# Early slots of a gated expert kernel: a second bank for layer 2, weight splits two loads behind, and the first main slot's weights in the early stream

## The chip, the core and the metric

The kernel runs on one core of a Trainium2 chip. Its time is device microseconds of one launch. The kernel before takes 796.64 us, the median of three runs (796.41 to 796.94).

## The reference

Random-feature attention over 8 batches, 8 heads, 576 positions and 64 channels makes x (8 x 576 tokens of 512). A gate then picks one of 8 experts for each token, and the token goes through that expert's two layers.

```python
def phi(x):
    proj = np.einsum('bhsd,df->bhsf', x, w_phi)          # 128 features
    proj = proj - np.max(np.abs(proj), axis=-1, keepdims=True)
    return np.concatenate([np.exp(proj), np.exp(-proj)], axis=-1)
q_p, k_p = (phi(q), phi(k))
kv = np.einsum('bhsf,bhsd->bhfd', k_p, v)
z = np.sum(k_p, axis=2)
x = np.einsum('bhsf,bhfd->bhsd', q_p, kv) / (np.einsum('bhsf,bhf->bhs', q_p, z)[..., None] + 1e-06)
...
for b in range(8):
    prev_e = -1
    for s in range(576):
        fresh_e = int(np.argmax(logits[b, s]))           # logits = x @ w_gate
        e = fresh_e if s == 0 or local_gate[b, s] < 0.5 else prev_e
        prev_e = e
        p = softmax(logits[b, s])
        h = np.maximum(x[b, s] @ w1[e], 0.0)             # 512 -> 1024
        out[b, s] = p[e] * (h @ w2[e])                   # 1024 -> 512
```

## The kernel before, in words

**Three parts.** The attention front takes two batches at a time (`bp` 0 to 3) and leaves x in DRAM. The gate of a pair counts tokens per expert and scatters each token's number and probability into a list in DRAM (`lst`), ordered by expert. The expert part works in *slots*: a slot is one expert and 256 tokens of its list (`n=(2,)`, two units of 128 tokens), or 512 (`n=(2, 2)`, a quad, which is two groups of 256), or 128.

**Early and main slots.** Three slots are planned before all tokens are counted: two after the second pair, one after the third (`EARLY = 3`, `HALFWAY = 2`). They are named E1, E2 and E3 here (`e0`, `e1`, `f0` in the code). TensorE works on them from about 316 us, when the front is done, to about 396 us; in this time the last pair's gate and the plan of the main slots (`plan_main`) run on VectorE and GpSimd. The plan comes in two steps, both called `more()` from layer 2: the arithmetic and the read of the list (L619), and then two transposes on TensorE that turn the list (L632). Main slots follow; M1 and M2 are the first two, both quads, M1 of expert rows that the plan names.

**A slot.** Its tokens are gathered from DRAM (GpSimd), transposed on TensorE (`tokens`, L914) and written as xhi (ScalarE, L923) and xlo (VectorE, L924). fp32 products are made of three fp32r matmuls, high by high (L928), low by high (L929) and high by low (L930). Layer 1 makes four tiles, each of two of the eight blocks of hidden features, in two banks of `psl` by turns; each is evicted as hh (ScalarE, L963) and hl (VectorE, L964). Layer 2 makes one tile (128 tokens x 512) for each unit; VectorE scales it by the probability (y, L1015) and GpSimd scatters it to the output (L1018). Until the front's pools are closed, layer 2's tiles all use one bank, `psm4`; M1 and later slots have two more (`psr`).

**Weights.** A slot has eight pieces of 128x1024 fp32 (512 KB), four for each layer. SyncE loads a piece into a raw buffer (L851; the expert number is read into a SyncE register first). There are three raw buffers (`mxg`), and from `open_rest` on, that is from M1 on, another three (`ml1`) by turns. A loaded piece is *split*: ScalarE casts it to whi (L861), VectorE subtracts for wlo (L862; for E1, GpSimd). Split pieces take a place in a ring of 12, from `open_rest` on 13.

**The order of loads and splits.** `spare()` starts the next piece of the next slot when a place of the ring will be free: load, then split. It is called through `used()` each time a piece has been used up. `slots()` runs a list of slots; `self.coming` holds those whose pieces are still to come. The early slots are one such list and the main slots another, so M1's pieces start only after the last early slot's code. Each engine takes its instructions in one order, fixed when the kernel is built: a scheduler picks them by priority and by when operands should be there, so code order is not the order on an engine. `tc.issue_after(x)` forbids it to place an instruction ahead of x.

Of the kernel before, what the change touches and what calls it, by code (L numbers as in the profile page):

```python
# [27 lines left out]
WAIT = 4  # L28
PLACE = 16
LAG = 1  # L30
WE, WR, WL = 8, 4, 1
FILL = 6
KVLAG = 1
# [16 lines left out]
class Kernel:  # L50
# [9 lines left out]
    def run(self):  # L60
        nc, tc, A = self.nc, self.tc, self.A
        act, dve = self.act, self.dve
        with ExitStack() as root:
# [77 lines left out]
                for _ in self.last_gate:  # L141
                    pass
            no = lambda: None
            self.slots(self.eslots, soon=[no, self.fetched_last, go, no, go, no, go, rest], later=[[no, no, more]] * 2)
            back.close()
            self.open_rest(root)
            self.moe()
# [716 lines left out]

    def spare(self):

        while self.coming:
            s = self.coming[0]
            i = len(s.get("w", ()))
            if i == 8:  # L870
                self.coming.pop(0)
                continue
            if self.held < sum(n for _, n in self.wphases):
                self.load(s, i)
                self.split(s)
                self.held += 1
            return

    def used(self, n):
        for _ in range(n):  # L880
# [62 lines left out]
    def layer1(self, s, gi, between, soon=()):  # L943

        pe, act, dve = self.pe, self.act, self.dve
        xh, xl = s["x"][gi]
        w, last = s["w"], gi == len(s["n"]) - 1
        hp = self.ml1 if gi else self.mx2
        hh = hp.tile([128, 8, 256], F32R, name="hh", bufs=1)
        hl = hp.tile([128, 8, 256], F32R, name="hl", bufs=1)  # L950
        s.setdefault("h", []).append((hh, hl))
        if s["n"][gi] == 2:
            for f2 in range(4):
                t = self.psl.tile([128, 2, 256], F32, name="l1")
                wh, wl = w[f2]
                for j in (0, 1):
                    for d in range(4):
                        c = slice(d * 256 + j * 128, d * 256 + j * 128 + 128)
                        self.three(t[:, j, :], wh[:, c], wl[:, c], xh[:, d, :], xl[:, d, :], d == 0, d == 3)
                    if soon:  # L960
                        soon[2 * f2 + j]()
                hc = slice(2 * f2, 2 * f2 + 2)
                act.activation(hh[:, hc, :], t, AF.Relu)  # L963
                dve.scalar_tensor_tensor(hl[:, hc, :], t, 0.0, hh[:, hc, :].bitcast(F32), ALU.max, ALU.subtract)  # L964
                if between:
                    between.pop(0)()
                if last:
                    self.used(1)
                else:
                    self.spare()  # L970
            return []

        hs = self.ml1.tile([128, 1024], F32, name="hs", tag="hh", bufs=1)
        x = slice(0, 128)

        def turn(q):
            tt = self.turned()
            for j in (0, 1):
                f = q * 2 + j
                pe.transpose(tt[:, j, :], hs[:, f * 128:f * 128 + 128], self.ident)  # L980
            hc = slice(q * 2, q * 2 + 2)
            self.parts(s, hh[:, hc], hl[:, hc], x, tt[:, 0:2])
        for q in range(4):
            t = self.psl.tile([128, 256], F32, name="l1")
            for d in range(4):
                self.both(s, q, t, xh[:, d, x], xl[:, d, x], slice(d * 256, d * 256 + 256), d == 0, d == 3)
                if d == 0 and q > 1:
                    turn(q - 2)
            act.activation(hs[:, q * 256:(q + 1) * 256], t, AF.Relu)
            if between and q in (0, 2):  # L990
                between.pop(0)()
            self.used(1)
        return [lambda: turn(2), lambda: turn(3)]

    def layer2(self, s, gi, between, held=None):
# [2 lines left out]
        u0 = s["u"] + sum(s["n"][:gi])  # L998
        for k in range(s["n"][gi]):
            self.l2n = getattr(self, "l2n", 0) + 1  # L1000
            p = self.psr if hasattr(self, "psr") and self.l2n % 3 else self.psm4
            t = p.tile([128, DM], F32, name="l2")
            o = slice(k * 128, k * 128 + 128)
            for f in range(8):
                c = slice((f % 2) * DM, (f % 2) * DM + DM)
# [6 lines left out]
                    self.spare()  # L1012
            y = self.mx2.tile([128, DM], F32, name="yl", bufs=1) if held is not None else self.mx2.tile([128, DM], F32, name="y")
            u = u0 + k
            dve.tensor_scalar_mul(y, t, s["prob"][:, u:u + 1])  # L1015

            def put(y=y, at=s["tok"][:, u:u + 1]):
                ins = pool.indirect_dma_start(self.A["out"], bass.IndirectOffsetOnAxis(at, 0), y, None,  # L1018
# [8 lines left out]
    def slots(self, order, held=None, soon=(), later=()):  # L1027
        first = order[0]
        for g in range(len(first["n"])):
            for f in self.tokens(first, g):  # L1030
                f()
        self.held = len(first.get("w", ()))
        self.coming = list(order)
        for i, s in enumerate(order):
            while len(s.get("w", ())) < 8:
                self.spare()
            new = order[i + 1] if i + 1 < len(order) else None
            last = len(s["n"]) - 1
            for gi in range(last):
                self.layer1(s, gi, [])  # L1040
            between = self.tokens(new, 0, bool(soon) and i == 0) if new else []
            rest = self.layer1(s, last, between, () if i else soon)
            if i < len(later):
                rest = list(later[i])
            for f in between:
                f()
            for gi in range(last + 1):
                self.layer2(s, gi, rest, None if new else held)
            if new and len(new["n"]) == 2:
                for f in self.tokens(new, 1):  # L1050
                    f()
            s.clear()
# [135 lines left out]
```

## Time and profile before

| | us | share of the span |
|---|---|---|
| median of three runs | 796.64 | |
| profiled execution | 796.07 | |
| its span, first to last instruction | 794.0 | |
| TensorE busy | 767.4 | 97% |
| VectorE busy | 511.2 | 64% |
| ScalarE busy | 401.9 | 51% |
| GpSimd busy | 158.0 | 20% |

Times in views of the trace count from the start of the span. PE is TensorE's matmul, PEld its weight load, DVE VectorE, ACT ScalarE, POOL GpSimd, SPq SyncE's queue. A row of a timeline holds start, duration, engine, line, operation, written tile <- read tiles, sizes, count, and in brackets the idle time ahead of it and what ended it (a line name stands there for the operation that released it). L12 is line 12 of the kernel. A row of the windows view holds the stretch and its length, then for PE, PEld, DVE, ACT and POOL the busy time with the number of instructions, then the granted TensorE clock as a share of the full one, the share of DMA busy, and GB/s. A row of the waits view names who waits, for what, and then total time, count and longest wait. In a trace the layer tiles are all called `l` and the transposed tokens `tr`.

### The profile page before, as it was taken

To read this page: it belongs to the slowest core of one execution; us is meant where nothing else is said; L and a number is where in the kernel's file an instruction comes from. 1 tells how busy PE (TensorE), PEld (TensorE's weight loads), DVE (VectorE), ACT (ScalarE), POOL (GpSimd) and SP (SyncE) were. 2 spreads that over 40 slices of the span, in tenths; PEclk is the share of its full clock that TensorE was granted. 3 is DMA by queue.
4 is the path that set the end of the run, shared out by engine and by line. 5 is a ranking of instruction groups with operands and counts; after the bars stand their busy time and mean duration, and the time that the engine had idled before them with its cause. 6 is when DMAs were issued, how large, how long until landed. Compare 5 with 4: busy or idle time off the path is not lost.

```text
span 794.0 us, 23193 instructions
## 1 busy us (share of the span) xinstructions
PE 767.4 (97%) x9674; PEld 676.2 (85%) x9674; DVE 511.2 (64%) x939; ACT 401.9 (51%) x708; POOL 158.0 (20%) x166
## 2 busy tenths in 40 slices
PE   6999999999999999999899999999999999999993
PEld 5899988988888989988798997698988987689882
DVE  4677798789878886985742225544866824768621
ACT  4666566666687665544531114433745713757410
POOL 0000001200275132166121102102321311110100
PEclk9999999999999999999999999999999999999997
DMA  7655454454687721747922695733966679959300
GB/s 200 195 163 155 116 146 128 135 139 122 172 264 208 223 77 42 225 148 277 333 83 88 261 347 180 258 120 114 362 204 201 244 262 410 358 188 321 111 27 14
DMA packets 77227, 151.29 MB, mean 191 GB/s; under 512 B 8524, under 2 KB 50828, under 8 KB 77078
## 3 DMA queue, kind: packets, MB, share of 16 engines
q1 hardware_dynamic: 67424, 127.33, 49.6%
q0 software_dynamic: 7424, 20.08, 7.1%
q10 hardware_dynamic: 2272, 2.37, 0.9%
q8 instruction: 77, 1.26, 0.7%
q14 instruction: 30, 0.25, 0.1%
HBM read 128.21 MB, written 22.06 MB: 189 GB/s over the span
## 4 chain that ended last, share of the span: by engine, by line
PE 84%; DVE 5%; DMA 4%; issue 2%; ACT 1%; SPq 1%; another core or an unknown queue 0%; POOLq 0%; POOL 0%; DVEq 0%
PE l L928 15%; PE l L930 15%; PE l L929 15%; PE kvp L255 9%; PE nm L314 9%; PE pj L213 9%; PE qt L233 4%; PE l L941 4%; DMA wraw<-in_w1h 3%; PE tr L914 2%; DVE m L216 1%; PE nm L293 1%; DVE sb L218 1%; PE nm L281 1%; PE tr L980 1%
## 5 line engine op out<-in xcount | busy, mean ns | idle before, releaser
L861 ACT CAST whi<-wraw 128x1024 fp32r<-128x1024 f32 x136 | 142.2, 1048 | 155.9 <-PE l L930 68.9
L862 DVE TENSOR_TENSOR wlo<-wraw,whi 128x1024 fp32r<-128x1024 f32 x128 | 156.2, 1222 | 75.4 <-ACT whi L861 73.7
L928 PE MATMUL l<-xhi,whi 128*128 128x256 f32 x512 | 146.2, 285 | 1.0 <-DVE hl L964 1.0
L930 PE MATMUL l<-xhi,wlo 128*128 128x256 f32 x512 | 143.7, 281 | 0.0
L929 PE MATMUL l<-xlo,whi 128*128 128x256 f32 x512 | 143.6, 281 | 0.0
L216 DVE TENSOR_REDUCE m<-pj 128x8 f32<-128x1024 f32 x72 | 87.8, 1220 | 47.4 <-PE pj L213 46.8
L928 PE MATMUL l<-whi,hh 128*128 128x512 f32 x288 | 114.5, 398 | 2.7 <-DVE y L1015 1.7
L930 PE MATMUL l<-whi,hl 128*128 128x512 f32 x288 | 113.2, 393 | 0.6 <-DVE hl L964 0.6
L929 PE MATMUL l<-wlo,hh 128*128 128x512 f32 x288 | 112.7, 391 | 0.0
L236 ACT ACTIVATE qp<-qt 128x512 f32<-128x512 f32 x144 | 84.7, 604 | 52.5 <-PE qt L233 52.0
L222 ACT ACTIVATE kp<-sb 128x512 f32<-128x512 f32 x144 | 82.8, 622 | 50.4 <-DVE sb L218 44.1
L928 PEld LDWEIGHTS l<-xhi,whi 128*128 128x128 f32 x512 | 96.8, 189 | 3.5 <-DVE hl L964 1.5
L929 PEld LDWEIGHTS l<-xlo,whi 128*128 128x128 f32 x512 | 96.8, 189 | 0.4
L930 PEld LDWEIGHTS l<-xhi,wlo 128*128 128x128 f32 x512 | 96.9, 189 | 0.1
L213 PE MATMUL pj<-first,kq 64*128 64x128 f32 x1152 | 85.5, 289 | 6.8 <-DMA kq<-in_kqT 6.8
L218 DVE TENSOR_TENSOR sb<-pj,m 128x1024 f32<-128x1024 f32 x72 | 88.1, 1224 | 4.0
L1018 POOL DMA_INDIRECT out<-y,p_tokm x31 | 39.2, 1263 | 244.2 <-DVE y L1015 243.6
L314 PE MATMUL nm<-kvs,qp 128*64 128x74 f32 x2304 | 86.7, 228 | 0.3
L213 PEld LDWEIGHTS pj<-first,kq 64*128 64x128 f32 x1152 | 71.5, 191 | 12.1 <-issue 4.6
L314 PEld LDWEIGHTS nm<-kvs,qp 128*64 128x64 f32 x2304 | 79.3, 136 | 1.4 <-ACT kvs L295 0.5
L255 PE MATMUL kvp<-v,kp 128*64 128x65 f32 x2048 | 77.3, 225 | 0.0
L255 PEld LDWEIGHTS kvp<-v,kp 128*64 128x64 f32 x2048 | 67.7, 139 | 5.9 <-issue 5.7
(229 smaller groups left out, 1028.1 us busy)
## 6 DMA issues: line engine op xcount, KB each, us to landing
wraw<-in_w1h SPq DMA_DIRECT2D x68, 512.0 KB, 5.3
wraw<-in_w2h SPq DMA_DIRECT2D x68, 512.0 KB, 5.1
kq<-in_kqT SPq DMA_DIRECT2D x47, 384.0 KB, 3.9
v<-in_va SPq DMA_DIRECT2D x48, 195.0 KB, 3.7
xs<-xo SPq DMA_DIRECT2D x48, 128.0 KB, 2.4
whi<-in_w1h SPq DMA_DIRECT2D x8, 512.0 KB, 4.3
wlo<-in_w1h SPq DMA_DIRECT2D x8, 512.0 KB, 5.0
whi<-in_w2h SPq DMA_DIRECT2D x8, 512.0 KB, 10.4
```

Source lines behind the costliest of these rows:

```text
L213: self.last_pe = self.pe.matmul(t[:, h, i % 2, j, :], kq[r, j, s], self.w2[r], start=True, stop=True)
L216: dve.tensor_reduce(m, f, AX.X, ALU.max, apply_absolute_value=True)
L218: self.last_dve = dve.tensor_sub(sb.rearrange("p h c j f -> p (h c j) f"), f, m.unsqueeze(2).broadcast_to([128, 8, 128]))
L222: self.last_act = act.activation(kp[:, :, :, sg, :].rearrange("p c h f -> p h c f"), sb[:, :, :, 0], AF.Exp, scale=1.0 - 2 * sg)
L236: self.act.activation(qp[:, sg], t, AF.Exp, scale=1.0 - 2 * sg)
L255: self.pe.matmul(self.kvp[r, sg, h], self.ch[i]["kp"][:, h, sg, r], self.v(i, b)[:, h], start=first and n < 2, stop=last and n >= 6)
L314: self.pe.matmul(e["t"][r, c - c0, h, :], self.ch[i]["qp"][:, sg, h, q0 + r.start:q0 + r.stop], kvs[:, sg, h, :], start=sg == 0, stop=sg == 1)
L861: self.act.copy(hi, raw)
L862: (low or self.dve).tensor_sub(lo, raw, hi.bitcast(F32))
L928: mm(o, ah, bh, start=first, stop=False)
L929: mm(o, ah, bl, start=False, stop=False)
L930: self.last_pe = mm(o, al, bh, start=False, stop=last)
```

## The change

1. *Second bank.* In the early slots the first unit's layer-2 tile stays in `psm4`; the second unit's goes to `psb`, a bank of the attention front (tag `nm`) that is idle by then.
2. *Splits two loads behind.* `spare()` now queues each loaded piece in `pending` and splits it when `MLAG = 2` later loads have been issued (or, when nothing is left to load, one at each call). In the early slots a split is also bound to come after the latest hh and after the latest hl or y that the code has reached (`issue_after`). For the main slots the lag is 0, as before. A piece takes its place in the ring's count at its load.
3. *M1 in the early stream.* After the second step of the plan, called from E2's layer 2, M1 is added to `self.coming` of the early list, so its pieces follow E3's through the three raw buffers of `mxg`.

```diff
+MLAG = 2
...
-            self.slots(self.eslots, soon=[no, self.fetched_last, go, no, go, no, go, rest], later=[[no, no, more]] * 2)
+            def last():
+                more()
+                self.coming.append(self.qs[0])
+            self.last_h, self.last_d, self.pending = self.last_act, self.last_dve, []
+            self.slots(self.eslots, soon=[no, self.fetched_last, go, no, go, no, go, rest],
+                       later=[[no, no, more], [no, no, last]])
...
     def spare(self):
+        got = False
         while self.coming:
             s = self.coming[0]
-            i = len(s.get("w", ()))
+            i = len(s.get("w", ())) + len(s.get("raw", ()))
             if i == 8:
                 self.coming.pop(0)
                 continue
             if self.held < sum(n for _, n in self.wphases):
                 self.load(s, i)
+                if s["raw"]:
+                    self.pending.append(s)
+                self.held += 1
+                got = True
+            break
+        while len(self.pending) > (self.lag if got else max(len(self.pending) - 1, 0)):
+            s = self.pending.pop(0)
+            with ExitStack() as st:
+                if self.lag:
+                    st.enter_context(self.tc.issue_after(self.last_h.ins))
+                    st.enter_context(self.tc.issue_after(self.last_d.ins))
                 self.split(s)
-                self.held += 1
-            return
...
-                act.activation(hh[:, hc, :], t, AF.Relu)
-                dve.scalar_tensor_tensor(hl[:, hc, :], ...)
+                self.last_h = act.activation(hh[:, hc, :], t, AF.Relu)
+                self.last_d = dve.scalar_tensor_tensor(hl[:, hc, :], ...)
...
-            p = self.psr if hasattr(self, "psr") and self.l2n % 3 else self.psm4
-            t = p.tile([128, DM], F32, name="l2")
+            if hasattr(self, "psr"):
+                p, kw = self.psr if self.l2n % 3 else self.psm4, {}
+            else:
+                p, kw = (self.psb, dict(tag="nm")) if k else (self.psm4, {})
+            t = p.tile([128, DM], F32, name="l2", **kw)
...
-            dve.tensor_scalar_mul(y, t, s["prob"][:, u:u + 1])
+            self.last_d = dve.tensor_scalar_mul(y, t, s["prob"][:, u:u + 1])
...
-        self.held = len(first.get("w", ()))
+        self.held = len(first.get("w", ())) + len(first.get("raw", ()))
         self.coming = list(order)
+        self.lag = MLAG if soon else 0
```

The change lengthens the file, so a line of before stands some 8 to 24 lines later after it (L632 becomes L640, L862 L870, L924 L944, L928 to L930 L948 to L950, L964 L984, L1015 L1039).

**Where instructions move.** Three places, each before and after. In these rows a number behind a tile's name tells one tile of a name from another; it differs between the two programs for the same tile.

TensorE, E2's layer 2, at the end of its first unit. Before, `l_6723` is E3's first layer-1 tile and `l_6684` E2's second unit:

```order
L930 MATMUL l_6723<-xhi,wlo 128x256
L928 MATMUL l_6723<-xhi,whi 128x256
L929 MATMUL l_6723<-xlo,whi 128x256
L928 MATMUL l_6684<-whi,hh 128x512
L929 MATMUL l_6684<-wlo,hh 128x512
L930 MATMUL l_6684<-whi,hl 128x512
L632 MATMUL pt<-first,lr 128x40 x2
```

After, `l_6646` is E2's first unit, `l_6684` its second:

```order
L949 MATMUL l_6646<-wlo,hh 128x512
L950 MATMUL l_6646<-whi,hl 128x512
L948 MATMUL l_6646<-whi,hh 128x512
L949 MATMUL l_6646<-wlo,hh 128x512
L950 MATMUL l_6646<-whi,hl 128x512
L950 MATMUL l_6684<-whi,hl 128x512
L640 MATMUL pt<-first,lr 128x40 x2
L948 MATMUL l_6684<-whi,hh 128x512
```

Before, E3's first layer-1 tile filled the place between the two units, and the plan's transposes (L632) stood inside the second unit. After, the second unit follows the first directly, the transposes stand right behind its start, and all of E3's layer 1 comes after it.

VectorE, E3's layer 1. Before, `wlo_6962` and the further splits are M1's pieces, and `hl_6722` is E3's hidden tile:

```order
L862 TENSOR_TENSOR wlo_6962<-wraw_6959,whi_6961 128x1024
L964 SCALAR_TENSOR_TENSOR hl_6722<-l1_6723,hh_6721 128x512
L862 TENSOR_TENSOR wlo_6968<-wraw_6965,whi_6967 128x1024
L862 TENSOR_TENSOR wlo_6974<-wraw_6971,whi_6973 128x1024
L964 SCALAR_TENSOR_TENSOR hl_6722<-l1_6750,hh_6721 128x512
L862 TENSOR_TENSOR wlo_6980<-wraw_6977,whi_6979 128x1024
L862 TENSOR_TENSOR wlo_6986<-wraw_6983,whi_6985 128x1024
L964 SCALAR_TENSOR_TENSOR hl_6722<-l1_6777,hh_6721 128x512
```

After, `y_6741` is E2's second unit, the splits are M1's, and `hl_6747` is E3's hidden tile:

```order
L1039 TENSOR_SCALAR y_6741<-l2_6684,p_probe_4777 128x512
L870 TENSOR_TENSOR wlo_6726<-wraw_6707,whi_6725 128x1024
L870 TENSOR_TENSOR wlo_6738<-wraw_6715,whi_6737 128x1024
L984 SCALAR_TENSOR_TENSOR hl_6747<-l1_6748,hh_6746 128x512
L870 TENSOR_TENSOR wlo_6778<-wraw_6723,whi_6777 128x1024
L984 SCALAR_TENSOR_TENSOR hl_6747<-l1_6781,hh_6746 128x512
L870 TENSOR_TENSOR wlo_6811<-wraw_6735,whi_6810 128x1024
L984 SCALAR_TENSOR_TENSOR hl_6747<-l1_6814,hh_6746 128x512
```

Before, two splits stand between one hl and the next; after, two ahead of the first hl and one between the others.

VectorE, from E3's layer 2 to M1. Before, `l2_6831` and `l2_6861` are E3's two units, `xlo_6913` and `xlo_6929` M1's first and second 256 tokens; `wlo_7075`, `wlo_7108`, `wlo_7141` and `wlo_7042` take the places of E3's last four pieces:

```order
L862 TENSOR_TENSOR wlo_7075<-wraw_7072,whi_7074 128x1024
L1015 TENSOR_SCALAR y_6856<-l2_6831,p_probf_6045 128x512
L924 TENSOR_TENSOR xlo_6913<-tr_6914,xhi_6912 128x4x128
L924 TENSOR_TENSOR xlo_6913<-tr_6921,xhi_6912 128x4x128
L862 TENSOR_TENSOR wlo_7108<-wraw_7105,whi_7107 128x1024
L862 TENSOR_TENSOR wlo_7141<-wraw_7138,whi_7140 128x1024
L862 TENSOR_TENSOR wlo_7193<-wraw_7190,whi_7192 128x1024
L1015 TENSOR_SCALAR y_6886<-l2_6861,p_probf_6045 128x512
L924 TENSOR_TENSOR xlo_6929<-tr_6930,xhi_6928 128x4x128
L924 TENSOR_TENSOR xlo_6929<-tr_6937,xhi_6928 128x4x128
L862 TENSOR_TENSOR wlo_7042<-wraw_7039,whi_7041 128x1024
```

After, `l2_6880` and `l2_6918` are the two units, `xlo_6970` M1's first 256 tokens (two tiles), and the splits are those that take the places of E3's last pieces (`wlo_7075` to `wlo_7042`) and one more of M2 (`wlo_7233`):

```order
L870 TENSOR_TENSOR wlo_6892<-wraw_6874,whi_6891 128x1024
L1039 TENSOR_SCALAR y_6913<-l2_6880,p_probf_6045 128x512
L870 TENSOR_TENSOR wlo_7075<-wraw_7072,whi_7074 128x1024
L870 TENSOR_TENSOR wlo_7108<-wraw_7105,whi_7107 128x1024
L870 TENSOR_TENSOR wlo_7141<-wraw_7138,whi_7140 128x1024
L1039 TENSOR_SCALAR y_6943<-l2_6918,p_probf_6045 128x512
L944 TENSOR_TENSOR xlo_6970<-tr_6978,xhi_6969 128x4x128
L870 TENSOR_TENSOR wlo_7042<-wraw_7039,whi_7041 128x1024
L870 TENSOR_TENSOR wlo_7233<-wraw_7230,whi_7232 128x1024
L944 TENSOR_TENSOR xlo_6970<-tr_6971,xhi_6969 128x4x128
```

Before, the first 256 tokens of M1 were ready for matmuls between E3's two units; after, both their tiles come behind the second unit's y, and two splits stand between them.

More of the change, by code (lines that the diff above doesn't have):

```diff
@@ L962, in layer1 @@
                 hc = slice(2 * f2, 2 * f2 + 2)
-                act.activation(hh[:, hc, :], t, AF.Relu)
-                dve.scalar_tensor_tensor(hl[:, hc, :], t, 0.0, hh[:, hc, :].bitcast(F32), ALU.max, ALU.subtract)
+                self.last_h = act.activation(hh[:, hc, :], t, AF.Relu)
+                self.last_d = dve.scalar_tensor_tensor(hl[:, hc, :], t, 0.0, hh[:, hc, :].bitcast(F32), ALU.max, ALU.subtract)
                 if between:
```

## Prediction

> **What bounds the kernel now.** I read the page first (busy shares and the chain that ended last), then busy time by window around the early slots, then the timeline of each engine from 316 to 400 us.
>
> ```profile
> span 794.0 us, 23193 instructions
> PE 767.4 (97%) x9674; PEld 676.2 (85%) x9674; DVE 511.2 (64%) x939; ACT 401.9 (51%) x708; POOL 158.0 (20%) x166
> PE 84%; DVE 5%; DMA 4%; issue 2%; ACT 1%; SPq 1%; another core or an unknown queue 0%; POOLq 0%; POOL 0%; DVEq 0%
> 340.00:360.00 20.00, 19.10 (x131) 17.35 (x130) 17.91 (x76) 10.91 (x14) 13.01 (x12) 1.00 0.56 187
> 360.00:380.00 20.00, 17.84 (x118) 15.84 (x117) 10.60 (x13) 7.39 (x8) 9.79 (x8) 1.00 0.78 280
> 380.00:400.00 20.00, 18.79 (x110) 15.67 (x109) 15.29 (x18) 12.02 (x15) 6.06 (x6) 1.00 0.88 319
> 500.00:600.00 100.00, 99.98 (x668) 88.69 (x665) 58.51 (x66) 46.74 (x64) 20.26 (x16) 1.00 0.61 207
> ```
>
> TensorE (first number after the comma) is full from 500 us on, so a microsecond gained before M1 starts reaches the end undiminished, and nothing after it can be gained. Between 340 and 400 us it idles 0.90 + 2.16 + 1.21 = 4.3 us: that is what the change can win. Where:
>
> ```profile
> 349.56 0.47 PE L928 MATMUL l<-whi,hh 128*128 128x512 f32 x1 [0.90 <-DVE p_rim L607]
> 363.96 0.50 PE L928 MATMUL l<-whi,hh 128*128 128x512 f32 x1 [1.21 <-DVE y L1015]
> 378.43 0.38 PE L928 MATMUL l<-xhi,whi 128*128 128x256 f32 x1 [0.95 <-DVE hl L964]
> 387.15 0.50 PE L930 MATMUL l<-whi,hl 128*128 128x512 f32 x1 [0.63 <-DVE hl L964]
> 389.75 0.51 PE L928 MATMUL l<-whi,hh 128*128 128x512 f32 x1 [0.53 <-DVE y L1015]
> 395.18 0.39 PE L930 MATMUL l<-whi,hl 128*128 128x512 f32 x1
> 395.42 1.03 PE L914 MATMUL tr<-first,xg 128*128 128x128 f32 x8
> 396.20 0.37 PE L928 MATMUL l<-xhi,whi 128*128 128x256 f32 x1
> 345.00 1.20 DVE L862 TENSOR_TENSOR wlo<-wraw,whi 128x1024 fp32r<-128x1024 f32 x1
> 348.68 0.73 DVE L1015 TENSOR_SCALAR y<-l,p_probe 128x512 f32<-128x512 f32 x1
> 349.40 0.67 DVE L964 SCALAR_TENSOR_TENSOR hl<-l,hh 128x512 fp32r<-128x512 f32 x1
> 362.02 1.22 DVE L862 TENSOR_TENSOR wlo<-wraw,whi 128x1024 fp32r<-128x1024 f32 x1 [0.87 <-ACT whi L861]
> 363.16 0.74 DVE L1015 TENSOR_SCALAR y<-l,p_probe 128x512 f32<-128x512 f32 x1
> 376.54 1.23 DVE L862 TENSOR_TENSOR wlo<-wraw,whi 128x1024 fp32r<-128x1024 f32 x1 [1.07 <-ACT whi L861]
> 377.68 0.69 DVE L964 SCALAR_TENSOR_TENSOR hl<-l,hh 128x512 fp32r<-128x512 f32 x1
> ```
>
> All five waits are for VectorE, which is late because a result (y, hl) stands behind a weight split (L862), and the split behind its load. At 363.96 and 389.75 the wait is for the one layer-2 bank; at 378.43 and 387.15 for hl behind a split. The last PE row is the first matmul of M1, 396.20: the point that the change must move. Counted from matmul start to matmul start (a restart also costs 0.1 to 0.2 us) the five take 1.1, 1.4, 1.1, 1.3 (E3's layer 2 has a second, shorter one) and 0.8 us.
>
> **The change part by part.** No instruction is added or removed on any engine; order, banks and buffers change.
>
> *Second bank.* E2's and E3's second units go to the other bank, so the waits of 363.96 and 389.75 go: 1.4 + 0.8, and about 0.3 of restarts. The first, at 349.56, only changes its name. The order now puts two matmuls of E2's second unit ahead (0.5 us done early), then the third layer-1 tile, which needs hl of the first; that hl stands behind three splits and a y as before (345.00 to 349.40), because the planning arithmetic in front of them waits for the same counts. I take it as unmoved: at best it goes (-1.1), at worst the split that now stands inside that arithmetic delays it by one split (1.2).
>
> *Splits two loads behind.* E3's eight splits keep their places up to 363 us; two of them and all of M1's follow later. E3's first loads move behind SyncE's register loads of the plan (from 331 to 347 us). That costs nothing: layer 1 of E3 starts near 367 and the pieces are split by then; without that cover it would be 16 us.
>
> *M1's pieces in the early stream.* These rows say when they come now, and how long a load takes:
>
> ```profile
> 319.35 0.36 SPq L851 DMA_DIRECT2D wraw<-in_w1h  x1
> 322.91 1.05 ACT L861 CAST whi<-wraw 128x1024 fp32r<-128x1024 f32 x1 [0.83 <-DMA wraw<-in_w1h]
> 365.39 2.04 SPq L851 DMA_DIRECT2D wraw<-in_w1h  x4
> 370.64 1.05 ACT L861 CAST whi<-wraw 128x1024 fp32r<-128x1024 f32 x1 [0.27 <-DMA wraw<-in_w1h]
> 375.46 1.05 ACT L861 CAST whi<-wraw 128x1024 fp32r<-128x1024 f32 x1 [1.24 <-DMA wraw<-in_w1h]
> 375.50 8.39 SPq L851 DMA_DIRECT2D wraw<-in_w1h  x4
> SPq L851 <- PE pt L632: 2.0, 1, 2.0
> SPq L851 <- DMA lr<-lst,p_rim: 1.0, 1, 1.0
> 358.48 1.31 POOL L619 DMA_INDIRECT lr<-lst,p_rim  x1 [0.31 <-issue]
> 364.85 0.41 PE L632 MATMUL pt<-first,lr 40*128 40x40 f32 x2
> ```
>
> M1's first load waited for the plan's transposes (L632) and left at 365.39. Alone, a load takes 3.6 us to its cast (319.35 to 322.91). In the burst of 365.39 the second (issued 0.6 later) takes 4.7, the fourth (issued at about 367.1) 8.4. In the change each load leaves when one of three raw buffers is free, so at most three are in flight, beside the token gathers: between 3.6 and 8.4, and I take 4.6, nearest to the second of the burst. [...]
>
> With 4.6 the splits follow each other by some 2.5 us: the last of E3's at 367.0, M1's first (free at 363.2, loaded by 367.0, behind a y) at 369.2, M1's second (issued 365.2, cast 369.8 to 370.9) at 372.0. The hl of E3's first layer-1 tile stands right behind that one: ready at 372.7, where TensorE wants its bank at 372.4. So of the 1.1 us of 378.43, 0.8 is won. The hl's of the later tiles come in time, so 387.15 goes: 1.3. The plan's transposes are now reached near 361.6; the list landed at about 363.3 before (SyncE's 2.0 us wait for L632 began there), issued at 358.48. The scatters start some 1.5 us earlier and the list read 3 to 4, so I take no wait; with the list unmoved it costs 1.7.
>
> So E3's layer 2 ends at 395.42 - (0.5 + 1.4 + 0.8 + 1.3 + 0.8 + 0.3) = 390.3 and, since the eight transposes between its units (0.8 by the 395.42 row) now stand behind it, at 389.5.
>
> *The boundary to M1* takes much of this back. Before, the first 256 tokens were turned between the two units and their parts were ready at 391. Now all are turned after both, and VectorE's order is: third released split, y, first xlo, two more splits, second xlo.
>
> ```profile
> 391.46 1.05 ACT L861 CAST whi<-wraw 128x1024 fp32r<-128x1024 f32 x1 [1.56 <-PE l L930]
> 395.66 1.05 ACT L861 CAST whi<-wraw 128x1024 fp32r<-128x1024 f32 x1 [0.33 <-PE l L930]
> 396.61 1.06 ACT L923 CAST xhi<-tr 128x512 fp32r<-128x512 f32 x2
> 395.36 1.23 DVE L862 TENSOR_TENSOR wlo<-wraw,whi 128x1024 fp32r<-128x1024 f32 x1 [0.21 <-ACT whi L861]
> 396.51 0.75 DVE L1015 TENSOR_SCALAR y<-l,p_probf 128x512 f32<-128x512 f32 x1
> 397.22 1.29 DVE L924 TENSOR_TENSOR xlo<-tr,xhi 128x512 fp32r<-128x512 f32 x2
> ```
>
> These casts wait for the second unit's matmuls to free E3's pieces, 1.4 us apart (391.46, then two more, then 395.66), the last 0.5 us after the last matmul began. In the change the fourth starts at 389.7, the third at 388.3, whose split takes VectorE to 390.5. Then y to 391.2; the first xlo to 392.0 (its cast, behind the fourth, ends at 391.3); two splits at 1.15 to 394.2; the second xlo to 394.9; four transposes more on TensorE (0.4) and M1's layer 1 goes on at 395.4. By then two of its matmuls (0.24) and four transposes of M2 (0.4) are done. The second of the two splits needs M2's sixth load, issued when M1's last split ends (about 384.8) with four ahead: landed near 390.3, cast by 392.4, in time by 0.7 us.
>
> Sum: 396.2 + 0.6 - 395.4 = 1.4 us. The profiled execution took 796.07 us, of which the span is 794.0, so 794.7; it lay 0.57 under the median of the runs, so 795.2. About 0.2% (1.6 us) is what a measurement of this kernel can tell from no change: the forecast lies just inside.
>
> **The rivals.**
> - *More is won.* Either the wait of 349.56 goes with the others (1.1), or M2's two splits don't hold the second xlo (2.3: it would follow the first). For: VectorE is idle for most of the 10 us that follow its split at 331 in the new order, so the planning could begin earlier. Against: its counts come from TensorE's place, which moves little, and the order fixes the two splits. Gain 2.5 to 4.8, centre 793.3.
> - *No change to be seen.* The loads come 1.4 us later than I put them, by slower transfers beside the gathers or by the list unmoved. For: the burst's third and fourth loads. Gain 0 +- 0.8: 796.6.
> - *Slower: the three raw buffers become the bound.* M1 had six buffers before, three of them opened by the release of the old pools; now three carry it. If a round trip is the 8.4 us of the burst, M1's second split ends 3.8 us later, TensorE waits that long for hl in E3's layer 1, and the later tiles add a little. From 6.0 us the gain is gone, from 7.6 it is slower by over 0.2%; at 8.4, 2.4 us: 799.0. Against: the burst had up to six weight loads in flight, not three.
> - *The lag does nothing.* If splits stay where they are, only the banks and the boundary count: that is the forecast with the 1.1 us of 378.43 kept, within the second rival.
>
> **How the numbers follow.** Forecast 0.45 (gain 0.6 to 2.2, 794.4 to 796.0), more is won 0.20, no change 0.23, slower 0.12. Faster by over 0.2% is the whole of "more is won" and not quite half of the forecast: 0.40; slower by over 0.2% 0.12; the rest, 0.48, lies within. The range leaves out the best part of the first rival and most of the third: 793.0 to 798.0.
>
> **What would show it.** In the profile after: no wait of PE for y at E2's and E3's second units; the wait near 350 us now on hl; one short wait for hl in E3's layer 1; M1's loads from about 363 us; E3's last layer-2 matmul near 389.2; then a wait of some 3.8 us in all around M1's transposes, on DVE, with M1's layer 1 running from 395.4. Casts waiting for DMA far beyond 5 us after the issue, with PE waiting for hl by 2 us or more, would show the third rival; a first layer-1 matmul of M1 well under 394, the first.

## The result and the profile after

The changed kernel takes 801.4 us, the median of eight runs (799.31 to 805.26); the kernel before took 796.94 beside it. The ratio is 1.0067 (95% interval 1.0052 to 1.0082): slower by some 0.7%, 5 us, where 1.4 us less was forecast. The profiled execution took 805.26 us, the slowest of the eight; its span is 9.3 us longer than that of before. So its waits show the mechanism, and their sum is that of a bad run.

The page's first line and the windows around the early slots, after (columns as before):

```profile
span 803.3 us, 23192 instructions
340.00:360.00 20.00, 18.83 (x134) 17.31 (x133) 17.55 (x77) 8.96 (x11) 12.64 (x12) 1.00 0.62 191
360.00:380.00 20.00, 16.58 (x101) 13.91 (x100) 11.41 (x14) 9.58 (x11) 9.04 (x8) 1.00 0.87 275
380.00:400.00 20.00, 15.90 (x87) 13.32 (x85) 13.88 (x14) 11.11 (x13) 1.98 (x2) 1.00 0.93 326
400.00:420.00 20.00, 18.97 (x138) 18.68 (x139) 8.22 (x12) 5.54 (x10) 4.87 (x5) 0.83 0.36 118
```

From 340 to 400 us TensorE idles 8.7 us (before: 4.3), in the next 20 us another 1.0, and there the granted clock is 0.83. Timeline of TensorE, its waits and the row that takes M1's layer 1 up for good:

```profile
351.56 0.39 PE L948 MATMUL l<-xhi,whi 128*128 128x256 f32 x1 [1.17 <-DVE hl L984]
362.55 0.51 PE L948 MATMUL l<-whi,hh 128*128 128x512 f32 x1 [1.03 <-ACT hh L983]
363.91 0.50 PE L950 MATMUL l<-whi,hl 128*128 128x512 f32 x1 [0.63 <-DVE hl L984]
378.12 0.39 PE L948 MATMUL l<-xhi,whi 128*128 128x256 f32 x1 [1.76 <-DVE hl L984]
381.72 0.39 PE L948 MATMUL l<-xhi,whi 128*128 128x256 f32 x1 [0.51 <-DVE hl L984]
400.15 0.33 PE L934 MATMUL tr<-first,xg 128*128 128x128 f32 x1 [3.74 <-DVE y L1039]
403.62 1.12 PE L934 MATMUL tr<-first,xg 128*128 128x128 f32 x4 [0.88 <-DVE xlo L944]
404.39 0.56 PE L949 MATMUL l<-xlo,whi 128*128 128x256 f32 x1
```

The waits for y between the units of E2 and E3, and those for hl inside E3's layer 2, are gone. In their place stand one for hh and one for hl in E2's layer 2, two for hl in E3's layer 1, and 4.6 us around M1's transposes. Their causes are in the order of ScalarE and VectorE and in the loads (an SPq row can hold several issues and starts at the first; 369.51 is the second of the four of 367.51):

```profile
355.02 0.33 SPq L859 DMA_DIRECT2D wraw<-in_w1h  x1
367.51 7.39 SPq L859 DMA_DIRECT2D wraw<-in_w1h  x4
369.51 0.33 SPq L859 DMA_DIRECT2D wraw<-in_w1h  x1
387.44 3.27 SPq L859 DMA_DIRECT2D wraw<-in_w1h  x4
360.95 1.05 ACT L869 CAST whi<-wraw 128x1024 fp32r<-128x1024 f32 x1 [2.54 <-DMA wraw<-in_w1h]
361.90 0.59 ACT L983 ACTIVATE hh<-l 128x512 fp32r<-128x512 f32 x1
375.15 1.05 ACT L869 CAST whi<-wraw 128x1024 fp32r<-128x1024 f32 x1 [1.89 <-DMA wraw<-in_w1h]
394.36 1.05 ACT L869 CAST whi<-wraw 128x1024 fp32r<-128x1024 f32 x1 [2.07 <-DMA wraw<-in_w1h]
397.13 1.99 ACT L869 CAST whi<-wraw 128x1024 fp32r<-128x1024 f32 x2 [0.23 <-DMA wraw<-in_w1h]
376.23 1.23 DVE L870 TENSOR_TENSOR wlo<-wraw,whi 128x1024 fp32r<-128x1024 f32 x1 [1.70 <-ACT whi L869]
377.38 0.68 DVE L984 SCALAR_TENSOR_TENSOR hl<-l,hh 128x512 fp32r<-128x512 f32 x1
396.93 2.50 DVE L870 TENSOR_TENSOR wlo<-wraw,whi 128x1024 fp32r<-128x1024 f32 x2 [0.27 <-ACT whi L869]
399.35 0.75 DVE L1039 TENSOR_SCALAR y<-l,p_probf 128x512 f32<-128x512 f32 x1
```

Three pictures of the same thing: something that TensorE waits for stands on its engine behind a split whose load has not landed. At 361 us it is E2's last hh, behind E3's fourth piece, which found a raw buffer only at 355.02 and was cast 5.9 us later. At 377 it is E3's hl behind M1's second piece, issued at 369.51 and cast 5.6 us later. At the boundary it is y behind three splits of M2, whose first load left at 387.44 and was cast 6.9 us later. In each case the load both left late and took longer than alone (3.6 us in the kernel before, 319.35 to 322.91). And then the clock:

```profile
398.00:400.00 2.00, 0.00 (x0) 0.00 (x0) 1.95 (x3) 1.61 (x3) 0.00 (x0) 1.00 1.03 336
400.00:402.00 2.00, 1.85 (x13) 1.85 (x13) 2.00 (x4) 1.93 (x3) 1.32 (x2) 0.72 0.95 334
406.00:408.00 2.00, 2.00 (x13) 2.00 (x12) 0.08 (x1) 0.00 (x0) 0.46 (x1) 0.57 0.78 215
408.00:410.00 2.00, 2.00 (x20) 2.00 (x19) 0.43 (x1) 0.60 (x1) 0.00 (x0) 1.00 0.18 72
```

Behind the wait of 3.74 us the granted clock is 0.50 for 6.8 us, until about 407.7. From 404.39 to 407.73 TensorE starts 15 matmuls of layer 1 in 3.34 us, the next 15, at 1.00, in 1.77: by an estimate from these two 1.6 us are lost. Layer 1 of M1 goes on 8.2 us later than before (404.39 against 396.20) with two matmuls done (0.24): 8.2 - 0.2 + 1.6 = 9.6, near the 9.3 of the spans.

### The profile page after: what moved, and what is told of

The parts are those of the page before. It is cut to its first block, busy times and chain, and to the rows that moved or that the text cites. A ratio compares the mean times of both kernels' runs of the same rounds, so it can differ in the third digit from the quotient of the medians.

```text
span 803.3 us, 23192 instructions
## 1 busy us (share of the span) xinstructions
PE 771.7 (96%) x9674; PEld 679.9 (85%) x9674; DVE 512.2 (64%) x939; ACT 402.0 (50%) x708; POOL 156.4 (19%) x166
## 4 chain that ended last, share of the span: by engine, by line
PE 82%; DVE 6%; DMA 5%; issue 2%; ACT 2%; SPq 1%; POOL 0%; another core or an unknown queue 0%; POOLq 0%; ACTq 0%; DVEq 0%
PE l L948 15%; PE l L950 14%; PE l L949 14%; PE kvp L263 9%; PE nm L322 9%; PE pj L221 8%; PE qt L241 4%; PE l L961 4%; DMA wraw<-in_w1h 2%; PE tr L934 2%; DMA wraw<-in_w2h 2%; DVE wlo L870 1%; DVE m L224 1%; PE nm L301 1%; ACT whi L869 1%
## 5 line engine op out<-in xcount | busy, mean ns | idle before, releaser
L870 DVE TENSOR_TENSOR wlo<-wraw,whi 128x1024 fp32r<-128x1024 f32 x128 | 156.2, 1223 | 77.3 <-ACT whi L869 75.7
L948 PE MATMUL l<-xhi,whi 128*128 128x256 f32 x512 | 147.3, 288 | 3.5 <-DVE hl L984 3.4
L950 PE MATMUL l<-xhi,wlo 128*128 128x256 f32 x512 | 144.3, 282 | 0.0
L948 PE MATMUL l<-whi,hh 128*128 128x512 f32 x288 | 114.2, 397 | 1.0 <-ACT hh L983 1.0
L950 PE MATMUL l<-whi,hl 128*128 128x512 f32 x288 | 113.2, 393 | 0.6 <-DVE hl L984 0.6
L948 PEld LDWEIGHTS l<-xhi,whi 128*128 128x128 f32 x512 | 97.6, 191 | 6.3 <-DVE hl L984 4.3
L950 PEld LDWEIGHTS l<-xhi,wlo 128*128 128x128 f32 x512 | 97.5, 190 | 0.0
L984 DVE SCALAR_TENSOR_TENSOR hl<-l,hh 128x512 fp32r<-128x512 f32 x64 | 43.9, 686 | 49.4 <-ACT hh L983 49.3
```

The source lines that it names most:

```text
L870: (low or self.dve).tensor_sub(lo, raw, hi.bitcast(F32))
L948: mm(o, ah, bh, start=first, stop=False)
L950: self.last_pe = mm(o, al, bh, start=False, stop=last)
```

## The experiments

Ratios are to the kernel before, run beside on the same chip. The runs fell on chips of two kinds: on some the kernel before takes 796 to 797 us, on two 809 to 810. On these TensorE idles near 350 us without a cause that the profile names (below), and ratios from there are not compared with those of the others. e11, e1b and e3b are e11b, e1 and e3 on the second of these two.

| run | what it is | before, us | kernel, us | ratio (95%) |
|---|---|---|---|---|
| first comparison | the change | 796.94 | 801.40 | 1.0067 (1.0052 to 1.0082) |
| again | the change | 796.25 | 803.40 | 1.0100 (1.0080 to 1.0120) |
| e8_hold | + M2's splits bound (VectorE) | 796.25 | 799.35 | 1.0054 (1.0034 to 1.0074) |
| e9_lag0_hold | the same, no lag | 796.25 | 801.37 | 1.0077 (1.0057 to 1.0097) |
| e7_idle | the kernel before, TensorE held up | 796.25 | 819.40 | one run |
| again2 | the change | 796.16 | 802.84 | 1.0079 (1.0061 to 1.0096) |
| e11b_hold2 | + M2's splits bound (both engines) | 796.16 | 797.56 | 1.0018 (1.0007 to 1.0029) |
| e14_late_m1 | e11b + 5 raw buffers, M1's splits late | 796.16 | 796.48 | 1.0003 (0.9989 to 1.0018) |
| e15_best | e14, E1 to E3 split at once, plan's second step later | 796.16 | 801.88 | 1.0066 (1.0047 to 1.0086) |
| e10_raw5_hold2 | e11b + 5 raw buffers | 796.13 | 794.34 | **0.9974** (0.9962 to 0.9986) |
| e16_six | e14, six of M1's splits before M1, plan's second step later | 796.13 | 795.85 | 0.9990 (0.9979 to 1.0002) |
| e1_bank | bank alone | 810.01 | 812.45 | 1.0024 (1.0007 to 1.0042) |
| e2_lag0 | the change, no lag | 810.01 | 811.99 | 1.0024 (1.0009 to 1.0039) |
| e3_nojoin | the change, M1 not joined | 810.01 | 811.35 | 1.0018 (1.0001 to 1.0036) |
| e5_raw5 | the change, 5 raw buffers | 810.01 | 811.16 | 1.0017 (1.0002 to 1.0032) |
| e11_hold2 | as e11b | 808.78 | 808.00 | 0.9993 (0.9972 to 1.0013) |
| e12_bank_hold2 | bank + M2's splits bound | 808.78 | 809.61 | 1.0012 (0.9998 to 1.0026) |
| e1b_bank | bank alone | 808.78 | 812.58 | 1.0036 (1.0021 to 1.0051) |
| e3b_nojoin | as e3 | 808.78 | 811.08 | 1.0025 (1.0005 to 1.0044) |

again2, e11b, e14, e15, e10 and e16 ran on the same chip.

**One part less.** e1_bank is the kernel before with the diff's bank lines; the others are the change with

```diff
-MLAG = 2                                # e2_lag0
+MLAG = 0
-                self.coming.append(self.qs[0])          # e3_nojoin
+                pass
-        rp = self.ml1 if hasattr(self, "ml1") and self.rk % 2 else self.mxg      # e5_raw5
+        m = [0, 2][hasattr(self, "mraw")]     # mraw: two more, from open_main on
+        rp = self.mraw if self.rk % (3 + m) >= 3 else self.mxg
```

> The kernel before with the second bank alone (the early slots' second unit in the idle bank; loads, splits and M1 as before). If the bank was sized rightly and the loss lies in the loads, the two waits for y (1.21 and 0.53 us) go and the kernel takes 794.5 to 796.3 us. If the bank itself does the harm (units run ahead and their results pile up on VectorE at the boundary to M1), it takes 797.5 us or more.

> The changed kernel with MLAG = 0: each piece is split right behind its load and bound to nothing; the bank and M1's early loads stay. If the lag and its bindings are the cause, E3's first loads leave near 331 us again, the waits near 362 us (1.03 and 0.63) go and it takes 796.5 to 798 us. If the three raw buffers are the cause whatever the lag, M1's loads still take 7 to 9 us each and it stays within 1.5 us of 801.4.

> The changed kernel without its third part: M1 stays out of the early list; bank, lag and bindings stay. If M1's loads through three raw buffers are the cause, M1's loads leave in a burst near 365 us, the two waits for hl in E3's layer 1 (1.76 and 0.51) go, the wait at the boundary is under 2 us, the clock stays at 1.00 and it takes 796 to 798 us. If the lag is the cause, it takes 799.5 us or more.

> The changed kernel with five raw buffers instead of three from the end of the attention front on (two new ones, in place of the three that M1 and later slots had besides). If the number of buffers holds M1's loads back, each load leaves some 5 us earlier, the waits for hl in E3's layer 1 go, and it takes 796 to 798.5 us. If the transfers themselves are the limit (they share the DMA engines with the gathers), more in flight only makes each longer and it stays within 1.5 us of 801.4.

These four ran on a chip of the other kind, and separate nothing: they lie within 0.0007 of each other. The timeline of TensorE (e1_bank) shows how the chip differs, with idle time that no operation ends (`issue`: the view names nothing that TensorE waited for):

```profile
352.22 0.28 PE L930 MATMUL l<-xhi,wlo 128*128 128x256 f32 x1 [1.03 <-issue]
```

One thing they do say: the bank alone is no gain there (1.0024, and 1.0036 in e1b, where 0.999 to 1.001 was expected). In both e1 and e1b y stands behind M2's splits at the boundary, a wait of 1.2 us.

**The boundary.** e8 binds M2's splits (`last_x` is M1's latest xlo), e9 has MLAG = 0 besides, and e7 prices the clock:

```diff
+                elif s is self.qs[1]:                                    # e8, e9
+                    st.enter_context(self.tc.issue_after(self.last_x.ins))
-            self.dve.tensor_sub(lo[:, :, o], ...)                        # e7, on the kernel before
+            more = dict(m8=6, m12=9, m14=12, m16=15).get(s["name"], 0) if o.start == 128 else 0
+            for _ in range(1 + more):
+                self.dve.tensor_sub(lo[:, :, o], ...)
```

> The changed kernel once more, unedited, to stand beside the variants on their chip. By either theory its ratio to the kernel before is 1.005 to 1.008 as in the first comparison. If the loss depends on where the loads, the gathers and the plan happen to meet on a chip, the ratio differs from chip to chip by more than the intervals.

> The changed kernel with one more binding: M2's splits may not stand ahead of M1's xlo on an engine (issue_after the last xlo of M1), so at the boundary VectorE's order is y, y, four xlo, then M2's splits. Theory boundary: M2's splits, which wait for loads of 7 us, stand ahead of y and of the xlo that TensorE waits for (3.74 and 0.88 us) and the long wait halves the granted clock for 8 us. Then the two waits shrink to under 1.5 us together, the clock stays 1.00 and the time falls to 796.5 to 798 (ratio 1.000 to 1.0015). Rival, raw buffers: M1 has too few pieces for layer 1 at that point anyway, the wait only changes its name, ratio 1.004 or more.

> As the last one, and with MLAG = 0, so that E3's loads leave near 331 us again and M1's follow them at once: bank, M1 in the early list and the binding of M2's splits stay. Theory boundary plus late loads: both causes are gone, the bank's gain stays, ratio 0.997 to 0.999, the fastest of the three. Rival, the order on VectorE without the lag brings back the splits ahead of hl: no better than the last one, ratio 1.000 to 1.003.

> The kernel before with TensorE held up on purpose in four later slots: M1's successor quad m8 and the pairs m12, m14 and m16 write the low part of their last transposed tile 6, 9, 12 and 15 times more on VectorE (0.6 us each, the same values), so that TensorE idles once in each, by some 1, 3, 4.5 and 6 us. Theory clock: behind the short waits the granted clock stays 1.00, behind those of 4 us and more it is 0.5 for 6 to 8 us, so the longer waits cost 3 to 4 us beyond themselves. Rival: the dip after the boundary was chance, the clock stays 1.00 behind all four.

e8 won 0.0046 of the 0.0100, less than expected. The wait for y fell to 0.41, but M2's four casts still stood ahead of xhi on ScalarE. The first two waited there 2.61 and 1.21 us for their loads, the next two followed at once, and xhi came behind them; the binding had moved the wait from one engine's queue to another's (TensorE and ScalarE, e8):

```profile
397.36 0.58 PE L950 MATMUL l<-xhi,whi 128*128 128x256 f32 x1 [2.61 <-ACT xhi L945]
390.82 1.05 ACT L869 CAST whi<-wraw 128x1024 fp32r<-128x1024 f32 x1 [2.61 <-DMA wraw<-in_w1h]
393.08 1.04 ACT L869 CAST whi<-wraw 128x1024 fp32r<-128x1024 f32 x1 [1.21 <-DMA wraw<-in_w1h]
396.24 0.58 ACT L945 CAST xhi<-tr 128x512 fp32r<-128x512 f32 x1
```

e9 was a miss. Without the lag TensorE came to the plan's transposes before the list had landed. The first read of the list waited 2.92 us on GpSimd until a split on VectorE had ended, and the last left at 358.88, against 355.08 in the change:

```profile
365.26 0.33 PE L640 MATMUL pt<-first,lr 40*128 40x40 f32 x1 [4.35 <-DMA lr<-lst,p_rim]
```

e7 did not give the four waits that were meant: only two places made TensorE wait, 5.42 us at the first, and 6.01 with 3.58 behind it at the second. But the kernel's own wait for y in E2's layer 2 came out at 1.87 us there (1.21 before). This wait and the 5.42, each with windows (e7):

```profile
363.57 0.51 PE L930 MATMUL l<-whi,hh 128*128 128x512 f32 x1 [1.87 <-DVE y L1017]
364.00:366.00 2.00, 2.00 (x8) 1.39 (x7) 0.31 (x2) 0.00 (x0) 1.43 (x2) 0.69 0.34 123
366.00:368.00 2.00, 2.00 (x7) 1.52 (x6) 0.00 (x0) 0.00 (x0) 1.39 (x3) 0.50 0.98 250
572.82 0.58 PE L931 MATMUL l<-xlo,whi 128*128 128x256 f32 x1 [5.42 <-DVE xlo L926]
570.00:574.00 4.00, 1.18 (x5) 1.18 (x6) 3.97 (x7) 0.00 (x0) 1.01 (x1) 0.50 0.93 320
574.00:578.00 4.00, 4.00 (x27) 4.00 (x26) 3.83 (x6) 0.70 (x1) 0.00 (x0) 0.70 0.33 129
```

In these windows the clock goes down to 0.50, where the kernel before has 1.00 (360 to 370 and 570 to 580 us); behind the 5.42 us it stays there past the wait's end, until about 576.4. Even the 1.87 us were followed by 3.4 us at 0.50, where the expectation had 1.00 behind short waits. The kernel took 23.2 us more than before: the three long waits make 15.0, and the 13.8 us in which TensorE worked at 0.50 add some 6.5, by an estimate from the 3.34 us for 1.77 of the first comparison. What the other profiles show of the clock is under the last heading.

**Both queues.** e11 binds on both; e12 is the bank with these bindings, without lag and join.

```diff
-            self.act.copy(hi[:, :, o], t)
+            self.last_xh = self.act.copy(hi[:, :, o], t)
...
+                elif s is self.qs[1]:
+                    st.enter_context(self.tc.issue_after(self.last_xh.ins))
+                    st.enter_context(self.tc.issue_after(self.last_x.ins))
```

> The changed kernel with M2's splits bound behind M1's last xhi on ScalarE and behind M1's last xlo on VectorE (with the binding on VectorE's side alone, the casts of M2 stayed ahead of xhi on ScalarE and waited there for their loads, 2.6 us). Theory boundary: the waits around M1's transposes fall from some 5.6 us (in the rerun of the changed kernel) to 1.5 to 2, no clock dip follows, and what is left of the loss is the late loads in E2 and E3: ratio to before 1.001 to 1.004. Rival, M1's own pieces come too late for its layer 1: the wait moves on to M1's layer 1, ratio 1.006 or more.

> The kernel before with the second bank and the same two bindings of M2's splits; loads, splits of E3 and M1 as before (no lag, M1 not in the early list). Theory: the two waits for y go (1.7 us) and the boundary keeps some 1.5 us, less than the bank wins: ratio 0.997 to 0.9995. Rival, VectorE's order in E3's layer 1 (two splits between one hl and the next) takes more when E3 starts earlier: ratio 1.000 to 1.002.

> [...] Theory: the two waits for y go and M2's splits take most of it back at the boundary: ratio 0.999 to 1.001. Rival, the bank alone makes the loss of the changed kernel: 1.004 or more.

> The bank and the lag without M1 in the early list, once more. Theory: the lag's late loads of E3 cost the waits in E2's layer 2 (1 to 1.7 us), M1's loads leave in a burst through six buffers as before: ratio 1.001 to 1.004. If joining M1 to the early list costs nothing, it is as slow as the changed kernel, 1.006 to 1.010.

Again a chip of the other kind. Within it the bindings are worth 0.0024 on the bank alone (e1b to e12; the two intervals overlap); e12 still does not beat the kernel before, though a gain was expected of it. With lag and join the kernel is level with before.

**The three places priced on one chip.** e14 has e11b's bindings, keeps M1's splits back until E3's last hl, and has e5's five raw buffers with at most five pieces waiting for their split; e15 is e14 with E1's to E3's pieces split at once and the plan's second step called one place later. The main lines:

```diff
+            if self.lag and hasattr(self, "qs") and self.pending[0] is self.qs[0] and not self.e3done:    # e14: e3done is set behind E3's last hl
+                break
...
-        while len(self.pending) > (self.lag if got else max(len(self.pending) - 1, 0)):                # e15
+        while len(self.pending) > (0 if got else max(len(self.pending) - 1, 0)):
...
-                       later=[[no, no, more], [no, no, last]])
+                       later=[[no, no, more], [no, no, no, last]])
```

> The changed kernel unedited, as the measure for the three that follow on this chip: ratio 1.006 to 1.010 where the kernel before takes 796 us; on a chip where it takes 809 us, nearer to 1.003, since waits of that chip near 355 us let the loads catch up.

> The changed kernel with M2's splits bound behind M1's xhi and xlo, on the chip of the rerun. Theory: the boundary is the largest of the three places, 3.5 to 5 us with the clock dips; the ratio is 0.004 to 0.006 below that of the rerun. Rival: M1's late pieces are the larger, the ratio is less than 0.002 below.

> As the last one, with M1's splits kept back until E3's last hl and five raw buffers instead of three so that M1's loads can still run ahead. Theory: the waits for hl in E3's layer 1 (2.5 and 0.5 us in the first rerun) go, and M1's eight splits fit into E3's layer 2 (10 of 11 us of VectorE): 0.002 to 0.004 below the last one, near 0.999 to 1.001. Rival: M1's first pieces come too late and TensorE waits for them in M1's layer 1, no better than the last one.

> As the last one, but E1's to E3's pieces are split right behind their loads (so that E3's loads leave near 331 us), and the second step of the plan is called one place later in E2's layer 2. Theory: the waits in E2 for a late hh and hl go too; what is left is the wait for the plan's arithmetic near 350 us (1 us) and 0.4 us at the boundary: ratio 0.995 to 0.998, faster than both kernels. Rival: TensorE comes to the plan's transposes before the list has landed and waits there 2 to 4 us: 0.999 to 1.002.

The binding on both queues takes 0.0061 off, 4.9 us, as expected: the boundary is the largest place. Rows of TensorE, first three of again2, then two of e11b:

```profile
377.38 0.43 PE L948 MATMUL l<-xhi,whi 128*128 128x256 f32 x1 [2.42 <-DVE hl L984]
398.99 0.33 PE L934 MATMUL tr<-first,xg 128*128 128x128 f32 x1 [2.56 <-DVE y L1039]
402.45 0.33 PE L934 MATMUL tr<-first,xg 128*128 128x128 f32 x1 [1.62 <-DVE xlo L944]
...
377.55 0.58 PE L951 MATMUL l<-xhi,whi 128*128 128x256 f32 x1 [3.24 <-DVE hl L987]
396.86 0.33 PE L937 MATMUL tr<-first,xg 128*128 128x128 f32 x1 [0.41 <-DVE y L1042]
```

2.56 and 1.62 became 0.41; the wait for hl in E3's layer 1 stayed. e14 took that away too, and then waited 1.59 us for y behind M1's last two splits. e15 was a clear miss, and shows what the lag is for: split at once, five pieces of E3 stand in VectorE's order inside the planning arithmetic, ahead of y and hl (three do in the change). The list lands late as well: its last read left GpSimd at 362.96, against 355.22 in again2, with 5.71 us of idle time ahead of the first for which the view names nothing, so why is open (VectorE, first and last of the five and the hl; TensorE):

```profile
344.76 1.20 DVE L872 TENSOR_TENSOR wlo<-wraw,whi 128x1024 fp32r<-128x1024 f32 x1
349.64 1.20 DVE L872 TENSOR_TENSOR wlo<-wraw,whi 128x1024 fp32r<-128x1024 f32 x1
351.43 0.67 DVE L991 SCALAR_TENSOR_TENSOR hl<-l,hh 128x512 fp32r<-128x512 f32 x1
352.15 0.39 PE L955 MATMUL l<-xhi,whi 128*128 128x256 f32 x1 [2.38 <-DVE hl L991]
368.12 0.30 PE L640 MATMUL pt<-first,lr 40*128 40x40 f32 x1 [3.03 <-DMA lr<-lst,p_rim]
```

**Buffers or order.** e10 is e11b with e5's five buffers. e16 is e14 with six of M1's splits ahead of the boundary, the last two bound behind M1's xhi and xlo, and the later call of the plan:

```diff
-            if self.lag and hasattr(self, "qs") and self.pending[0] is self.qs[0] and not self.e3done:
+            if self.lag and hasattr(self, "qs") and self.pending[0] is self.qs[0] and not (self.e3done and len(self.qs[0]["w"]) < 6):
```

> The changed kernel with M2's splits held back (as e11b) and five raw buffers instead of three; M1's splits stand between the hl's of E3's layer 1 as in the change. If three raw buffers are the bound, five let M1's loads leave 5 us earlier, the wait for hl in E3's layer 1 (3.2 us in e11b) goes, and it is as fast as e14: ratio 0.999 to 1.001. If the order is the cause (a split ahead of hl whatever the buffers) and the transfers only get longer, a wait of 2 us or more stays: 1.001 to 1.003.

> e14 with two edits: only six of M1's eight splits come before the boundary, its last two stand behind M1's xlo (they are wanted 20 us later), and the second step of the plan is called one place later in E2's layer 2. Theory: the wait for y at the boundary falls from 1.6 to 0.4 us and the wait for the list from 1.9 to 0.5: some 2.5 us less than e14, ratio 0.996 to 0.998, faster than both kernels. Rival: the late list only moves on (M1's gathers land later, TensorE waits for them): 0.999 to 1.001.

With its one edit, the buffers, e10 decides for them. SyncE's queue, VectorE and TensorE:

```profile
334.80 4.88 SPq L861 DMA_DIRECT2D wraw<-in_w1h  x4
354.48 6.40 SPq L861 DMA_DIRECT2D wraw<-in_w1h  x4
372.44 0.69 DVE L989 SCALAR_TENSOR_TENSOR hl<-l,hh 128x512 fp32r<-128x512 f32 x1 [2.71 <-ACT hh L988]
350.26 0.39 PE L953 MATMUL l<-xhi,whi 128*128 128x256 f32 x1 [1.86 <-DVE p_rim L615]
363.51 0.30 PE L640 MATMUL pt<-first,lr 40*128 40x40 f32 x1 [1.69 <-DMA lr<-lst,p_rim]
392.26 0.33 PE L939 MATMUL tr<-first,xg 128*128 128x128 f32 x1 [0.41 <-DVE y L1044]
```

E3's loads leave at 334.80, M1's first at 354.48 instead of 367.51. In E3's layer 1 VectorE now waits for hh (2.71 us idle) and TensorE does not wait for VectorE; no cast of weights waits for its load from 345 to 405 us. Three waits of TensorE are left, 4.0 us in all. It takes 794.34 us, 0.26% less than the kernel before, where a ratio of 0.999 to 1.001 was expected: it beats both, though it has five raw buffers in the main slots where before has six. e16 lost the two waits that it was made for (list, and y at 0.41) and got a new one of 0.98 us for hl in M1's layer 1, with 1.88 for the plan's arithmetic. Its time can't be told from that of the kernel before, where a ratio of 0.996 to 0.998 was expected.

## Why the prediction was wrong

- *The waits for y go with the second bank; the first wait only changes its name.* Right: no wait between units, and 1.17 us for hl at 351.56.
- *E3's loads behind the register loads of the plan: "costs nothing".* The step that failed first. E3's pieces were not split by 367: its fourth was cast at 360.95 and the last at 369.84. The text looked for the wait in E3, where the weights are used; it came in E2 (1.03 and 0.63), because the cast stands in one queue with E2's eviction. And it set back the loads of M1, from 363.2 to 367.51 for the first and from 365.2 to 369.51 for the second.
- *A load takes 4.6 us.* Mis-sized, but by less (and the 4.6 would put M1's first load at 367.8, where the text has 367.0; its sum hangs on the second alone): M1's four pieces of layer 1 took 4.7 (at most), 5.6, 6.6 and 6.9 us, M2's first 6.9. Late start and longer transfer together brought M1's second cast to 375.15, where 369.8 stood, and the hl behind it to 377.38 plus its own 0.68, where 372.7 stood. The third rival had the mechanism (three raw buffers) with the wrong driver: it asked for 6 us a load, and did not see that the buffers already held E3 back. With five buffers (e10) E3's first five loads leave from 334.80 on, M1's first at 354.48, and E3's layer 1 has no wait. That is worth 0.0044 (e11b to e10, 3.5 us), E2's waits included.
- *The boundary: waits of some 3.8 us in all.* The size was about right (3.74 and 0.88), by luck, since the reason was another: the splits in front of y waited for M2's loads, since M1's last split, put at 384.8, began at 392.31. The text booked the wait inside a gain. The runs show it as the largest loss: 0.0061 (4.9 us, what follows of the clock included) with M2's splits bound behind M1's tokens.
- *The clock.* No term and no rival had it. The sum counted idle time at its length; in the first comparison the clock of 0.50 behind the 3.74 us cost some 1.6 us more (the estimate above).
- The chance of slower was 0.12, with 799.0 for it. That rival was priced in one place; the same lateness went on to M2's splits and the boundary, and the parts added up.

Still open: the shares of bank, lag and join one by one on a chip of the first kind, since the runs with one part less met the other kind. There the bank alone, the change without the lag and the change without the join all were 0.0018 to 0.0036 slower than before. Why the list lands late in e15 is open too.

## What to carry to other kernels

A split (or any operation that needs a transfer) that is moved in an order must be checked against everything behind it on each of its engines, not only against its own reader: here late loads stopped hh, hl, y, xhi and xlo in turn, and a binding on one engine only moved the wait to the other. When loads are moved to run ahead, count the buffers they run through by round trips under the traffic of that stage: two more buffers and two bindings turned 0.8% lost into 0.26% won. And a wait of TensorE should be costed with the clock in and behind it: here 0.50 came with some of the waits from 1.57 us (e1b) to 2.61 us (e8) and, on the chips of the first kind, with each of 3 us or more, and behind the 3.74 us it cost some 1.6 us more.

## What the hardware showed beside this

The granted clock from 300 to 780 us, in the profiles on chips where the kernel before takes 796 us: the stretches at 0.50 lasted 3.41, 6.83 or 13.65 us (read in windows of 0.1 us): 3.41 in again2, e8, e9 and e11b, 6.83 in the first comparison and e15, and 3.41, 6.83 and 13.65 in e7, the last with two waits of 6.01 and 3.58 us. Each began in a wait of TensorE or at most 1.2 us behind its end. One came with every other single wait of 3 us or more: 3.03 (e15), 3.24 (e11b), 3.74 (first comparison), 4.35 (e9) and 5.42 us (e7). Of the shorter ones 1.87 (e7), 2.42 (again2) and 2.61 us (e8) came with one, but not 1.97 (e9), 2.38 (e15), 2.50 and 2.63 (again), 2.56 (again2) and 2.68 us (e8), nor those of up to 1.9 us in e10, e14 and e16. On a chip of the other kind a wait of 1.57 us ending at 389.51 (e1b) was followed, from 389.86 to 393.25, by 16 matmuls of 128x256 of 0.39 to 0.41 us each, against 0.28 us behind them. So between 1.6 and 2.7 us the length of the wait alone did not tell in these runs which way it went.

The changed kernel's longest waits lay in this range and above it, 2.42 to 3.74 us in its three profiles, and its eight runs spread over 6 us, those of before over 1.6. That the clock makes this spread is likely, but not shown. Of again2, the window behind its wait of 2.42 us reads

```profile
378.00:380.00 2.00, 2.00 (x12) 2.00 (x11) 0.40 (x1) 1.48 (x2) 1.70 (x2) 0.50 1.11 385
```

Chips differ: the same kernel before takes 796 us on some and 809 to 810 on two. In seven of the eight profiles taken there TensorE idles near 350 us, 0.2 to 1.7 us at a time, with no cause that the view names, and in the eighth (e5) 7.9 us for the plan's arithmetic; VectorE stops in the same stretch, up to 1.8 us at a time in e1. The granted clock is 0.50 there for 6.8 to 13.7 us between 353 and 369 us. What delays the engines was not tried.
